# A causal and sink-window attention feeding a two-matmul FFN: one explicit list of pieces in place of generated interleaving

## The chip, the cores and the metric

The kernel runs on one core of one Trainium2 chip. The metric is device microseconds of one execution, as the median of several. Before the change it is 242.58 us (three runs, 242.34 to 242.89). The profile that is read below is one execution with a span of 241.1 us from the first to the last instruction.

Names used throughout: TensorE (PE) multiplies matrices, VectorE (DVE) and ScalarE (ACT) work on tiles and read the matmul results out of PSUM, GpSimd (POOL) works on tiles in SBUF and starts some transfers, SyncE (SP) starts most transfers. Each engine takes its instructions in the order in which the program lists them for it.

## The reference

Four batches, eight heads, 768 tokens, head size 64. Heads 0, 2 and 6 are "retrieval" heads with full causal attention. The others are "streaming" heads: a token sees the first four tokens and the last 64. The attention output of all heads is then put through an FFN of width 512, 2048, 512 with a PReLU between.

```python
scores = scale * np.matmul(q, k.transpose(0, 1, 3, 2))
rel = pos[:, None] - pos[None, :]
causal = rel >= 0
stream_keep = causal & (is_sink | (rel < window))       # n_sink = 4, window = 64
mask = np.where(is_retrieval, causal, stream_keep)      # per head
a = softmax(np.where(mask, scores, -1e9))
x = np.matmul(a, v)        # transposed and reshaped to (3072, 512)
h = x @ w_in               # (3072, 2048)
g = np.maximum(h, 0.0) + alpha * np.minimum(h, 0.0)
out = g @ w_out            # (3072, 512), float32
```

Inputs are float32; the kernel casts to bfloat16 and accumulates in float32.

## The kernel before

Heads are handled in 16 pairs n: four pairs per batch, in the order (0, 1), (2, 3), (6, 7), (4, 5). For the first eight pairs q and k are transposed on TensorE; for the others a transfer transposes them. The FFN takes tokens in eight groups t, of 512 and 256 tokens alternately, two per batch.

The pieces, cut to what matters:

```python
# PSUM: 8 banks of 128 x 512 float32, by fixed roles
BANK = {"sc0": 0, "sc1": 1, "mm2": 2, "m2": 3, "mm0": 4, "mm1": 5, "m0": 6, "m1": 7}

def Tq(n):      # transpose q of both heads (6 matmuls), then copy to qT
    tr = T_bank(natq.pop(n), ...)
    nc.scalar.copy(qT[n % NK][:, 0:S]..., in_order(tr[:, 0:S], T))          # L301

def Tk(n):      # transpose k of both heads (6 matmuls), then copy to kT, head by head
    ...         # copies: L314 (retrieval heads), L320 to L322 (streaming heads)

def S_retr(n, hh, m):                    # scores of a retrieval head, piece m
    ... nc.tensor.matmul(sc..., kt..., qt..., stop=not masked)              # L362
        if masked:   # n < 4: add -30000 where not causal, by a matmul
            nc.tensor.matmul(sc..., ident, nmr..., start=False, stop=True)  # L365
    nc.scalar.activation(e..., sc..., AF.Exp, scale=scale)                  # L370
    ... nc.vector.tensor_tensor(ej, ej, mask, op=ALU.mult)   # n >= 4       # L375

def S_stream(n, hh, m):                  # scores of a streaming head
    on_pe = n < 3 or n == 3 and hh == 1
    ... nc.tensor.matmul(sc..., kt..., qt..., start=True, stop=not on_pe)   # L393
        if on_pe:
            nc.tensor.matmul(sc..., ident, nms..., start=False, stop=True)  # L396
    nc.scalar.activation(slots, sc..., AF.Exp, scale=scale)                 # L400
    if not on_pe:
        nc.vector.tensor_tensor(slots, slots, factor, op=ALU.mult)          # L404
# n >= 8 has a streaming form of its own: L412, L415, L419, L420, L422

def AV(n, hh):                           # attention times values, then normalise
    ... nc.tensor.matmul(pav[:, i, :], e..., vv...)          # 27 or 13     # L467
    nc.vector.reciprocal(rcp, pav[:, :, D:D + 1])                           # L472
    nc.vector.tensor_tensor(xn[n]..., pav..., rcp..., op=ALU.mult)          # L473

def X(n):                                # transpose the output: TensorE or a transfer
    ... nc.tensor.transpose(tr..., nat[:, i, :], ident)      # 7            # L486
    nc.vector.tensor_copy(xT[:, n % 4, o:o + S], tr[:, 0:S])                # L487

def P1(t, f, cs=range(4), where=""):     # first FFN matmul: 4 or 8 matmuls per piece
    ... nc.tensor.matmul(psg..., w_in_b..., xT[:, c, o:o + w])   # c: pair  # L516
    nc.scalar.activation(neg, psg, AF.Relu, scale=-1.0)                     # L523
    nc.vector.scalar_tensor_tensor(g_buf..., neg..., oma..., psg...)        # L526

def P2(t, s, quarter, where=""):         # second FFN matmul: 4 matmuls per quarter
    ... nc.tensor.matmul(bank(po[t, s]), g_buf..., w_out_b[:, f, :])        # L536
    if quarter == 3:
        nc.scalar.copy(ot, bank(po.pop((t, s))))                            # L541
        (nc.gpsimd if t < 6 else nc.sync).dma_start(out[r:r + 128, :], ot)
```

Each piece issues its matmuls and what ScalarE and VectorE do with them in one go, so the order of pieces is the order of all engines. The order comes from loops. Batch 0 (n < 4) is written out, with 36 warming matmuls ahead of it:

```python
whole_q(0); whole_k(0)
for i in range(36):
    nc.tensor.matmul(warm[:, 0:128], ident, ident, start=True, stop=True)
Tq(0); Tk(0)
...
for n in range(4):      # scores of pair n, with AV and X of pair n - 1 and Tq, Tk of n + 1 between
    ...
AV(3, 1)
LEAD = 4
for f in range(2):
    P1(0, f, range(3), where="lead")     # over the pairs 0 to 2, before X(3)
X(3)
for f in range(2, LEAD):
    P1(0, f, range(3), where="lead")
nc.vector.tensor_scalar(mr, nmr, 0.0, None, op0=ALU.is_equal)               # L663
...                                      # the rest of P1(0, ...)
```

From pair 4 on, `seg_pieces(n)` gives the attention pieces of a pair, and FFN pieces of earlier tokens are laid between them by a budget, evenly from one batch's end to the next. Loads of pair n + 4 follow in a pair's loop, on SyncE; the weights are loaded by GpSimd in eight transfers after the casts of batch 0.

Of the kernel before, what the change touches and what calls it, by code (L numbers as in the profile page):

```python
# [8 lines left out]
AF = mybir.ActivationFunctionType  # L9
ALU = mybir.AluOpType  # L10
DT = mybir.dt


@with_exitstack
def kernel(
# [60 lines left out]
    BANK = {"sc0": 0, "sc1": 1, "mm2": 2, "m2": 3, "mm0": 4, "mm1": 5, "m0": 6, "m1": 7}  # L76

    def bank(tag):
        return P[:, BANK[tag], :]

    def bank_bf(tag):
        return P[:, BANK[tag], :].bitcast(bf16)

# [80 lines left out]
    def load(n):  # L164
        load_q(n)
        load_k(n)
        load_v(n)

    natq, natk = {}, {}
# [7 lines left out]


    def whole_q(n):
        nat = natq[n] = NAT0[0][n] if n < 4 else NATQ[n % 2]  # L180
        copy = nc.gpsimd.tensor_copy if 0 < n < 6 else nc.scalar.copy if 0 < n < CROSS else nc.vector.tensor_copy
        flat = qf[n % NF].rearrange("p a b d -> p (a b d)")[:, 0:12 * D]
        copy(nat.rearrange("p i (h d) -> p h i d", h=2), flat.rearrange("p (h i d) -> p h i d", h=2, d=D))
        if n >= CROSS:
            nc.sync.dma_start(qT[n % NK][:, 0:S].rearrange("p (i r) -> p i r", r=128),
                              nat.rearrange("p i c -> p (i c)"), transpose=True)

    def whole_k(n):
        if n < CROSS:
            natk[n] = NAT0[1][n] if n < 4 else NATK1[n % 2]  # L190
            for hh, h in enumerate(heads(n)):
                copy = nc.gpsimd.tensor_copy if 0 < n < 6 else nc.scalar.copy if n == hh == 0 else nc.vector.tensor_copy

                T = row_tokens(n, h)
                flat = kf[n % NF].rearrange("p a b d -> p (a b d)")[:, 6 * D * hh:6 * D * (hh + 1)]
                copy(natk[n][:, :, D * hh:D * (hh + 1)].rearrange("p (t i) d -> p t i d", t=T),
                     flat.rearrange("p (i t d) -> p t i d", t=T, d=D))
            return
        flat = NATK[n % 2]
        rows = flat.rearrange("p (h x) -> p h x", h=2)[:, :, 0:896].rearrange("p h (t c) -> p h t c", c=128)  # L200
        nc.vector.tensor_copy(rows[:, :, :, 0:D], kf[n % NF].rearrange("p t h d -> p h t d"))
        sinks(n, rows)
        for hh, h in enumerate(heads(n)):
            nt = 6 if RETR[h] else 7
            nc.sync.dma_start(kTs[n % NK][hh][:, 0:128 * nt].rearrange("p (i r) -> p i r", r=128),
                              flat[:, 896 * hh:896 * hh + 128 * nt], transpose=True)

    def whole_v(n):
        vv = vb[n % NV]
        (nc.gpsimd if n < 6 else nc.vector).tensor_copy(vv[:, :, :, 0:D], vf[n % NF])  # L210
        sinks(n, vv.rearrange("p t h c -> p h t c"))

    for i in range(NF):
        nc.vector.memset(vf[i][:, 6, :, :], 0.0)
    load_q(0)
    load_k(0)
    alpha_r = wpool.tile([16, 128], fp32, name="alpha_r")
    nc.scalar.dma_start(alpha_r, moe_alpha.rearrange("(a p) -> a p", p=128))
    for n in range(1, 4):
        load_q(n)  # L220
        load_k(n)
        load_v(n - 1)
    load_v(3)

    zero = const.tile([128, 1], bf16, name="zero")
    nc.vector.memset(zero, 0.0)
    one = const.tile([128, 1], bf16, name="one")
    nc.vector.memset(one, 1.0)
    ident = const.tile([128, 128], bf16, name="ident")
    make_identity(nc, ident)  # L230
    ident_f = const.tile([16, 16], fp32, name="ident_f")
    mr = const.tile([128, 5, 144], bf16, name="mr")
    mr_near = const.tile([128, 6, 208], bf16, name="mr_near")

    ms_near = const.tile([128, 3, 176], bf16, name="ms_near")
    ms = const.tile([128, 2, 192], bf16, name="ms")
    ms5 = const.tile([128, 2, 192], bf16, name="ms5")
    nmr = const.tile([128, 5, 144], bf16, name="nmr")
    nms = const.tile([128, 192], bf16, name="nms")
    nms6 = const.tile([128, 44], bf16, name="nms6")  # L240
    OUT = -30000.0


    nc.gpsimd.affine_select(nms, zero.to_broadcast([128, 192]), pattern=[[-1, 192]], base=63,
                            channel_multiplier=1, compare_op=ALU.is_ge, fill=OUT)
    nc.gpsimd.memset(nms[0:NSINK, 0:128], 0.0)
    nc.gpsimd.affine_select(nms, nms, pattern=[[1, 192]], base=0,
                            channel_multiplier=-1, compare_op=ALU.is_ge, fill=OUT)

    nc.gpsimd.tensor_copy(nms6, nms[:, 0:44])  # L250
    nc.gpsimd.memset(nms6[0:NSINK, 0:NSINK], OUT)

    nc.gpsimd.affine_select(nmr, zero.unsqueeze(1).to_broadcast([128, 5, 144]), pattern=[[-4, 5], [1, 144]], base=0,
                            channel_multiplier=-1, compare_op=ALU.is_ge, fill=OUT)

    nc.scalar.copy(kT_all[:, 2].rearrange("p h c -> p (h c)"), zero.to_broadcast([128, 2 * 7 * 128]))
    nc.vector.memset(kT_all[:, 0].bitcast(fp32), 0.0)
    nc.vector.memset(qT_all[:, :, S:S + 32].bitcast(fp32), 0.0)
    nc.gpsimd.memset(kT_all[:, 3].bitcast(fp32), 0.0)
    nc.vector.memset(kT_all[:, 1].bitcast(fp32), 0.0)  # L260
    nc.vector.memset(vb_all[:, :, :, :, D:D + 1], 1.0)
    ONES = 1.001937866210937
    nc.vector.memset(eR_all[:, :, FAR.RTOT:E_R].bitcast(fp32), ONES)
    eSv = eS_all[:, :, 0:6 * SLOT].rearrange("p n (s c) -> p n s c", c=SLOT)
    for i in range(NS):
        nc.vector.memset(eSv[:, i, :, 192:SLOT].bitcast(fp32), 0.0)
    nc.vector.memset(eS_all[:, :, 5 * SLOT + 192:6 * SLOT + 128].bitcast(fp32), ONES)
    nc.vector.tensor_copy(ident_f, ident[0:16, 0:16])

    w_in_b = wpool.tile([128, 4, d_ff], bf16, name="w_in_b")  # L270
    w_out_b = wpool.tile([128, 16, d_model], bf16, name="w_out_b")
    oma = wpool.tile([128, 16], fp32, name="oma")

    def load_w_in(lo, hi):
        nc.gpsimd.dma_start(w_in_b[:, :, lo:hi], moe_w_in[:, lo:hi].rearrange("(a p) f -> p a f", p=128))

    def load_w_out(n):
        nc.gpsimd.dma_start(w_out_b[:, 4 * n:4 * n + 4, :],
                            moe_w_out[512 * n:512 * (n + 1), :].rearrange("(a p) f -> p a f", p=128))


    n_misc = [0]

    def misc_tag():
        n_misc[0] += 1
        return f"m{n_misc[0] % 2}"

    def T_bank(nat, tag):
        tr = bank_bf(tag)
        for i in range(6):  # L290
            nc.tensor.transpose(tr[:, 128 * i:128 * (i + 1)], nat[:, i, :], ident)  # L291
        return tr
# [5 lines left out]
    def Tq(n):  # L298
        tr = T_bank(natq.pop(n), "mm0" if n < 4 else misc_tag())
        T = row_tokens(n)  # L300
        nc.scalar.copy(qT[n % NK][:, 0:S].rearrange("d (p t) -> d p t", t=T), in_order(tr[:, 0:S], T))  # L301

    def Tk(n):
        tr = T_bank(natk.pop(n), "mm1" if n < 4 else misc_tag())
        for hh, h in enumerate(heads(n)):
            T = row_tokens(n, h)
            rows = slice(64 * hh, 64 * hh + 64)
            kt = kTs[n % NK][hh][rows, :]
            src = in_order(tr[rows, 0:S], T)
            copy = nc.scalar.copy if n >= 4 and hh == 0 else nc.vector.tensor_copy  # L310
            if RETR[h]:
                cuts = [0, -(-256 // T), S // T] if n == 0 else [0, S // T]
                for lo, hi in zip(cuts, cuts[1:]):
                    copy(kt[:, 0:S].rearrange("d (p t) -> d p t", t=T)[:, lo:hi, :], src[:, lo:hi, :])  # L314
                continue
            slots = kt.rearrange("d (j m t) -> d j m t", j=7, t=T)
            a, first, z, last = NSINK // T, NSINK // T, 748 // T, 128 // T
            if n >= LAY:
                first, z, last = 0, 672 // T, 116 // T
            copy(slots[:, 0:6, a:last, :], src[:, first:z, :].rearrange("d (j m) t -> d j m t", j=6))  # L320
            nc.vector.tensor_copy(slots[:, 6, a:a + S // T - z, :], src[:, z:S // T, :])
            nc.vector.tensor_copy(slots[:, :, 0:a, :], src[:, 0:a, :].unsqueeze(1).to_broadcast([64, 7, a, T]))  # L322

    ebuf = {}
    n_e = [0, 0]

    def take_e(n, hh):
# [441 lines left out]
```

The softmax here doesn't subtract the row's maximum and nothing guards it: scores larger than these inputs give would overflow.

## Time and profile before

| what | value |
|---|---|
| time, median of 3 | 242.58 us (242.34 to 242.89) |
| span in the profile | 241.1 us, TensorE clock 1.000 |
| first transpose of real data | 5.69 us |
| last matmul ends | 237.80 us |
| costliest line of VectorE: L526 (PReLU) | 74.6 us busy, 128 pieces |
| costliest line of ScalarE: L523 (its ReLU) | 57.3 us busy, 96 pieces |
| costliest lines of TensorE: L516, L536 (FFN) | 95.4 and 92.0 us busy |
| moved by transfers | 36.25 MB, 90,513 packets |

How to read the views: a line of the groups gives the source line, engine, operation, the tiles with their shapes, a count, then the busy time, the mean length of one in ns, and the idle time of the engine just before it. The windows give every engine's busy time in a stretch of time. The waits give for which engine and line one engine stood idle. The chain of work that ended last goes backwards from the last instruction, at each step to what released it. Matmuls are pipelined: the mean length of one (379 ns for 512 columns) is more than the distance from its start to the next one's start.

### The profile page before, as it was taken

Reading aid. Unit: us, or ns where it says so; the run is one execution under the profiler, and the core shown is the slowest. Engines: PE = TensorE matmul, PEld = TensorE weight load, DVE = VectorE, ACT = ScalarE, POOL = GpSimd, SP = SyncE. Lnnn points to the kernel's source line nnn. Section 1 sums busy time; section 2 is a strip of 40 time slices with the busy share of each in tenths; the row PEclk is TensorE's granted clock in tenths of the full one; section 3 lists DMA queues with packets and bytes.
Section 4 is the critical chain, followed back from the end, with each engine's and each line's share of the span. In section 5 each row is a group of like instructions: output and inputs, shape, how many; then the busy total and the mean of one; then the engine's idle time right before and its main releaser. Section 6 shows DMA issues by size and latency. Waiting matters only on the chain.

```text
span 241.1 us, 5264 instructions
## 1 busy us (share of the span) xinstructions
PE 229.2 (95%) x2017; PEld 144.1 (60%) x2017; DVE 165.5 (69%) x405; ACT 144.1 (60%) x265; POOL 43.7 (18%) x90
## 2 busy tenths in 40 slices
PE   7799799989987999999999999999999999999994
PEld 6688545566756655455666655556666544465553
DVE  7688889768788867989577858884665465633410
ACT  5788358957855756776655557866564254523220
POOL 5668950641110100000000000000000000000000
PEclk9999999999999999999999999999999999999999
DMA  6999999999999999999999991603131101011112
GB/s 212 292 251 169 232 202 201 244 251 254 251 224 162 196 244 211 217 162 245 164 238 168 219 169 59 126 3 77 46 78 44 46 0 45 0 59 74 44 44 90
DMA packets 90513, 36.25 MB, mean 150 GB/s; under 512 B 77672, under 2 KB 88696, under 8 KB 90488
## 3 DMA queue, kind: packets, MB, share of 16 engines
q1 hardware_dynamic: 84504, 26.66, 56.9%
q0 software_dynamic: 5664, 8.91, 16.6%
q10 hardware_dynamic: 320, 0.34, 0.6%
q8 instruction: 16, 0.26, 0.5%
q14 instruction: 9, 0.07, 0.1%
HBM read 27.55 MB, written 6.29 MB: 140 GB/s over the span
## 4 chain that ended last, share of the span: by engine, by line
PE 84%; DVE 7%; ACT 6%; issue 1%; ACTq 0%; DVEq 0%
PE P L516 34%; PE P L536 31%; PE P L467 6%; PE P L362 5%; ACT eR L370 2%; PE P L412 2%; PE P L291 2%; ACT eS L400 2%; PE P L553 1%; DVE xn L473 1%; PE P L486 1%; DVE eS L404 1%; DVE g L526 1%; PE P L393 1%; ACT neg L523 1%
## 5 line engine op out<-in xcount | busy, mean ns | idle before, releaser
L526 DVE SCALAR_TENSOR_TENSOR g<-neg,oma,P 128x512 bf16<-128x512 f32 (+1 forms) x128 | 74.6, 610 | 43.2 <-ACT neg L523 41.6
L516 PE MATMUL P<-xT,w_in_b 128*128 128x512 bf16 (+1 forms) x512 | 95.4, 326 | 0.0
L536 PE MATMUL P<-w_out_b,g 128*128 128x512 bf16 x368 | 92.0, 379 | 0.0
L523 ACT ACTIVATE neg<-P 128x512 f32<-128x512 f32 x96 | 57.3, 598 | 51.5 <-PE P L516 46.9
L516 PEld LDWEIGHTS <-w_in_b 128*128 128x128 bf16 x512 | 48.0, 98 | 29.3 <-issue 0.5
L536 PEld LDWEIGHTS <-g 128*128 128x128 bf16 x368 | 33.9, 98 | 30.1
L370 ACT ACTIVATE eR<-P 128x488 bf16<-128x488 f32 (+4 forms) x63 | 38.4, 620 | 13.9 <-PE P L362 11.8
L544 POOL DMA_DIRECT2D out_dram<-ot x18 | 9.8, 544 | 134.0 <-ACT ot L541 134.0
L362 PE MATMUL P<-qT,kT 128*128 128x488 bf16 (+17 forms) x132 | 24.7, 273 | 1.5 <-ACT eS L400 0.6
L473 DVE TENSOR_TENSOR xn<-P,rcp 128x448 bf16<-128x448 f32 x32 | 20.0, 624 | 1.1
L541 ACT COPY ot<-P 128x512 f32<-128x512 f32 x23 | 13.5, 587 | 9.0 <-PE P L536 8.6
L362 PEld LDWEIGHTS <-kT 128*128 128x128 bf16 x132 | 11.5, 98 | 10.0 <-issue 0.8
L415 ACT ACTIVATE eS<-P 128x352 bf16<-128x352 f32 x30 | 13.9, 462 | 5.7 <-PE P L412 5.7
L400 ACT ACTIVATE eS<-P 128x384 bf16<-128x384 f32 (+1 forms) x25 | 13.2, 558 | 4.6 <-PE P L393 4.0
L467 PE MATMUL P<-vb,eS 128*128 128x65 bf16 x260 | 11.7, 193 | 2.5 <-DVE eS L404 1.3
L467 PEld LDWEIGHTS <-eS 128*128 128x128 bf16 x260 | 10.5, 97 | 5.3 <-DVE eS L404 1.5
L467 PEld LDWEIGHTS <-eR 128*128 128x128 bf16 x324 | 11.4, 97 | 2.5 <-DVE eR L375 0.9
L467 PE MATMUL P<-vb,eR 128*128 128x65 bf16 x324 | 12.1, 192 | 0.8 <-DVE eR L375 0.8
L375 DVE TENSOR_TENSOR eR<-eR,mr_near 128x128 bf16<-128x128 bf16 (+5 forms) x36 | 8.2, 240 | 6.7 <-ACT eR L370 6.7
L420 DVE TENSOR_TENSOR eS<-eS,ms_near 128x352 bf16<-128x352 bf16 x30 | 10.1, 338 | 3.8 <-ACT eS L415 3.6
L393 PE MATMUL P<-qT,kT 128*128 128x192 bf16 (+2 forms) x70 | 10.0, 234 | 0.8 <-ACT eR L370 0.6
L412 PEld LDWEIGHTS <-kT 128*128 128x128 bf16 x70 | 6.6, 98 | 6.4
(97 smaller groups left out, 187.3 us busy)
## 6 DMA issues: line engine op xcount, KB each, us to landing
qf<-in_q_dram SPq DMA_DIRECT2D x16, 384.0 KB
out_dram<-ot POOLq DMA_DIRECT2D x18, 256.0 KB, 3.1
vf<-in_v_dram SPq DMA_DIRECT2D x22, 192.0 KB
kf<-in_k_dram SPq DMA_DIRECT2D x21, 192.0 KB
w_in_b<-in_moe_w_in_dram POOLq DMA_DIRECT2D x4, 512.0 KB, 8.3
w_out_b<-in_moe_w_out_dram POOLq DMA_DIRECT2D x4, 512.0 KB, 19.9
kf<-in_k_dram SPq DMA_DIRECT2D x9, 196.0 KB
vf<-in_v_dram SPq DMA_DIRECT2D x9, 196.0 KB
```

The lines of the kernel that those rows point to most:

```text
L362: nc.tensor.matmul(sc[:, x, a - lo:z - lo], kt[:, 128 * j:128 * (j + 1)], qt[:, c:c + z - a], start=True, stop=not masked)
L370: nc.scalar.activation(e[:, lo:hi].rearrange("p (x c) -> p x c", x=len(parts)), sc[:, 0:len(parts), 0:(hi - lo) // len(parts)], AF.Exp, sc ...
L393: nc.tensor.matmul(sc[:, x, o:o + w], kt[:, 128 * j:128 * (j + 1)], qt[:, 124 * j:124 * j + w], start=True, stop=not on_pe)
L400: nc.scalar.activation(slots, sc[:, 0:len(thirds), 0:384].rearrange("p x (s c) -> p x s c", c=192), AF.Exp, scale=scale)
L415: nc.scalar.activation(slots, sc[:, 0:352].rearrange("p (s c) -> p s c", c=176), AF.Exp, scale=scale)
L467: nc.tensor.matmul(pav[:, i, :], e[:, o:o + 128], vv[:, j, hh, 0:D + 1], start=(m == 0), stop=(m == len(terms) - 1))
L473: nc.vector.tensor_tensor(xn[n][:, :, 64 * hh:64 * hh + 64], pav[:, :, 0:D], rcp.to_broadcast([128, NT, D]), op=ALU.mult)
L516: nc.tensor.matmul(psg[:, w * i:w * (i + 1)], w_in_b[:, a, 128 * fb:128 * (fb + 1)], xT[:, c, o:o + w], start=(c == 0), stop=(c == 3))
L523: nc.scalar.activation(neg, psg, AF.Relu, scale=-1.0)
L526: nc.vector.scalar_tensor_tensor(g_buf[t % 2][:, fb, 0:w], neg[:, c], oma[:, fb:fb + 1], psg[:, c], op0=ALU.mult, op1=ALU.add)
L536: nc.tensor.matmul(bank(po[t, s]), g_buf[t % 2][:, f, 128 * s:128 * (s + 1)], w_out_b[:, f, :], start=(f == 0), stop=(f == 15))
L541: nc.scalar.copy(ot, bank(po.pop((t, s))))
```

## The change

The pieces are split so that what TensorE does (capital letters in the list) and what ScalarE or VectorE does with the result (small letters) are separate items. All items, 1,063 of them, are called in the order of one list, which is written out. The order on each engine thus no longer follows from the order on another. PSUM banks are taken from a pool, by which was free longest, instead of by fixed roles.

Along with this:

- All masks of batch 0 are added on TensorE, also that of pair 3's first head.
- The first pair is loaded (q), cast, transposed and copied head by head.
- 26 warming matmuls instead of 36.
- The first six pieces of the first FFN matmul go in three parts: pairs 0 and 1, pair 2, pair 3.
- The mask factors mr (for L375) are built at the start rather than after batch 0.
- Loads, casts and mask building stand in the list too, so weights and pairs are loaded in another order.

The purpose is to keep TensorE busy where it waited for the other engines.

The core of the diff; the list is cut to its beginning and two later stretches:

```diff
+ORDER = """
+id zero kz3 qz0 nmr Lq0.0 sz2 Lk0 Ck0.1 warm kz0 ro Lq1 kz2 kz1 Lq0.1 Cq0.0 Tq0.0 Ck0.0 vo Cq1 gate mr Lk1 vz0 Cq0.1
+Lq2 vz1 La sz1 idf Tk0.0 tq0.0 tk0.0 Ck1.0 Tk0.1 S0.0.2 S0.0.0 Lv0 Tq0.1 s0.0.2 Lk2 Ck1.1 qz S0.0.1 tk0.1 Tk1 tq0.1
 ...
+S2.0.2 s2.1.1 Lk4 X1 tk3.0 wi1 x1 s2.0.2 S2.1.0 s2.1.0 A2.0 S3.0.1 nz1 Lq4 tk3.1 A2.1 Cv3 S3.0.0 wi2 Ck4.0 s3.0.1
+s3.0.0 a2.0 a2.1 P0.3.0 Lk5 S3.1.0 S3.1.1 X2 wi3 P0.2.0 Cq4 s3.1.1 one A3.0 x2 P0.1.0 s3.1.0 A3.1 P0.1.1 kfz2 P0.0.0
+P0.0.1 P0.3.1 Lv4 a3.0 P0.5.0 Ck4.1 a3.1 X3 ms P0.4.0 P0.2.1 P0.5.1 x3 P0.0.2 P0.4.1 p0.0 g0.0 P0.5.2 P0.3.2 nr p0.5
 ...
+g4.2 g4.11 p4.12 S14.0.4 a12.1 Lk15 m13.0.1 s14.0.4 O3.1.0 S14.1.1 Dq15 m13.0.0 P5.2 S14.0.0 P4.14 g4.12 m14.1.0 A13.0
 ...
+""".split()
 ...
-    BANK = {"sc0": 0, "sc1": 1, "mm2": 2, "m2": 3, "mm0": 4, "mm1": 5, "m0": 6, "m1": 7}
+    def take(*choices):
+        got = min((c for c in choices if all(age[b] >= 0 for b in c)), key=lambda c: max(age[b] for b in c))
+        for b in got:
+            age[b] = -1
+        return got
 ...
+    MISC = [(6,), (7,)]
+    SC = [(0,), (1,)]
+    SC2 = [(0, 1), (2, 3)]
+    FF = [(2,), (3,), (4,), (5,)]
+    LEAD = [(4,), (5,), (3,), (2,), (0,), (1,)]
+    TAIL = [(b,) for b in (2, 3, 4, 5, 0, 1, 6, 7)]
 ...
-        on_pe = n < 3 or n == 3 and hh == 1
 ...
+                nc.tensor.matmul(sc[:, x, o:o + w], kt[:, 128 * j:128 * (j + 1)],
+                                 qt[:, 124 * j:124 * j + w], start=True, stop=n >= 4)
+                if n < 4:
+                    nc.tensor.matmul(sc[:, x, o:o + w], ident, (nms6 if j == 6 else nms)[:, 0:w],
+                                     start=False, stop=True)
 ...
-        for i in range(36):
+        for i in range(26):
 ...
+    for i in range(2):
+        item(f"Lq0.{i}", nc.sync.dma_start, part_of(qf[0], i), dram(q, i * S * D, [[6 * D, 128], [1, 6 * D]]))
+        item(f"Cq0.{i}", cast_q0, i)
+        item(f"Tq0.{i}", lambda i=i: to_array(("q0", i), natq[0], MISC, i == 0))
+        item(f"tq0.{i}", put_q, ("q0", i), 0, slice(D * i, D * i + D), "AV"[i])
+        item(f"Tk0.{i}", lambda i=i: to_array(("k0", i), natk[0], [(4,), (5,)], i == 0))
+        item(f"tk0.{i}", put_k, ("k0", i), 0, i)
 ...
+            if t == 0 and f < 6:
+                for part, cs in enumerate((range(0, 2), range(2, 3), range(3, 4))):
+                    item(f"P0.{f}.{part}", P1, 0, f, cs, LEAD)
 ...
+    for name in ORDER:
+        I[name]()
```

The items: L loads, C casts, T and t transposes and their copies, S, s and m scores, exponentials and masks, A and a attention times values and its normalisation, X and x the transposes of the output, P, p and g the first FFN matmul, its ReLU and its PReLU, O and o the second FFN matmul and its copy out, wi and wo the weights. S4.1.2 is pair 4, second head, third piece; P0.3.1 is token group 0, piece 3, second part.

## The prediction

> **What bounds the kernel now.** I read the page first: busy shares, then the forty slices.
>
> ```profile
> PE 229.2 (95%) x2017; PEld 144.1 (60%) x2017; DVE 165.5 (69%) x405; ACT 144.1 (60%) x265; POOL 43.7 (18%) x90
> PE   7799799989987999999999999999999999999994
> ```
>
> A slice is 6.03 us. TensorE (PE) is full from the fourteenth slice on and has holes before. The busy share hides most of a hole, because a matmul's modelled end lies about 0.17 us after the next could have started. So I looked at start-to-start times instead, in the chain of work that ended last (start, length, what):
>
> ```profile
> 13.06 0.81 PE P L467 x27
> 80.61 0.87 PE P L516 x8
> 82.04 0.86 PE P L536 x4
> ```
>
> That is 30 ns for 65 columns, 109 ns for 256 and 216 ns for 512: columns divided by 2.4 GHz plus about 2.4 ns[...].
>
> This gives an account of the span. Summed over the groups by shape, the 2017 matmuls have 521,056 columns: 217.1 us, and 2017 x 2.4 ns adds 4.8. I count 222.4, because those under 65 columns don't fall below some 28 ns. The 36 warming matmuls (4,608 columns, 2.0 us) lie ahead of the first transpose, at 5.69 us. So 220.4 us of needed work stands between 5.69 and the last matmul's end at 237.80, which is 232.1 us. **TensorE idles 11.7 us in between**; another 3.3 us at the end are the last copy and store.
>
> Where? The same stages in the windows (length; busy and count by engine; clock; DMA share; GB/s):
>
> ```profile
> 5.60:30.60 25.00, 21.45 (x340) 18.33 (x341) 19.35 (x49) 16.80 (x23) 19.58 (x35) 1.00 1.13 237
> 30.60:42.00 11.40, 11.40 (x65) 5.47 (x63) 10.88 (x15) 8.14 (x14) 3.00 (x9) 1.00 1.22 199
> 42.00:78.00 36.00, 32.50 (x350) 22.30 (x349) 28.98 (x82) 25.80 (x50) 8.92 (x18) 1.00 1.14 231
> 78.00:187.00 109.00, 109.00 (x943) 66.19 (x942) 81.08 (x210) 70.04 (x142) 7.02 (x13) 1.00 0.79 148
> ```
>
> Start-to-start excess over 0.1 us adds up to about 5.3 us in the first stage (attention of batch 0), nothing in the second (first matmul of the FFN), about 4.9 in the third (batch 1), and one 0.14 us hole afterwards; the rest is the small per-matmul excess. The waits of TensorE, for 0 to 30 us and 42 to 78 us, name the causes (waited for: total, times, longest):
>
> ```profile
> PE P L467 <- DVE xn L473: 1.2, 2, 1.0
> PE P L393 <- ACT eR L370: 0.6, 1, 0.6
> PE P L362 <- DVE kT L314: 0.5, 1, 0.5
> ...
> PE P L467 <- DVE eS L404: 1.3, 2, 0.8
> PE P L486 <- DVE xn L473: 0.9, 1, 0.9
> PE P L467 <- DVE eR L375: 0.8, 1, 0.8
> ```
>
> These are queues on VectorE (DVE) and ScalarE (ACT) that stand in program order, not an engine at its limit: in 42 to 78 us DVE is 80% busy. The largest is around the only mask of batch 0 that VectorE still multiplies:
>
> ```profile
> 24.46 1.61 DVE L404 TENSOR_TENSOR eS<-eS,ms 128x768 bf16<-128x768 bf16 x1 [0.47 <-ACT eS L400]
> 26.00 0.19 DVE L472 RECIPROCAL rcp<-P 128x7 f32<-128x7 f32 x1
> 26.22 0.62 DVE L473 TENSOR_TENSOR xn<-P,rcp 128x448 bf16<-128x448 f32 x1
> ```
>
> The outputs of pair 2 have to queue behind 1.61 us of masking for pair 3; TensorE has a hole of 1.16 us before 26.91, then 0.61 and 0.37.
>
> **What the Trainium skill says.** "TensorE: Matmul & The Clock Gate", section "Back-to-back issue gap", gives N/2.4 + 2.5 ns for a warm array; the trace agrees (216 ns at 512). The same page, section "Architectural detail: the array is 16× 32×32, not 1× 128×128", has ScalarE and VectorE as strict first-in first-out; the lines just shown fit. "SBUF — State Buffer", section "SBUF: two separate sides", says VectorE and GpSimd exclude each other on a shared port pair. The 768-wide mask at 1.61 us, against 0.366 us for a 384-wide one, ran while GpSimd issued weight transfers (24.35 to 27.3 us), which agrees in direction. "Trace analysis", section "Identifying the Most-Contended Engine", says matmul busy time misleads: here 95% with 11.7 us idle.
>
> **The change, part by part.**
>
> *Work.* The mask of pair 3's first head goes to TensorE: 7 matmuls, 1,152 columns. The first pair is transposed head by head: 12 more transposes, 1,536 columns. Ten warming matmuls go: 1,280 columns, in time that is idle anyway. Needed work rises by 2,688 columns, 1.12 us, and 19 x 2.4 ns: **plus 1.2 us**, to 221.6. VectorE loses 1.61 and 0.36 us of masking, and gains one 64-partition copy of 768 columns (0.94 us by the L314 row).
>
> *Start.* The first q transfer is halved and its cast covers half the columns, so the first transpose may come around 5.3 us instead of 5.69: minus 0.4. But building all of mr (1.96 us at 31.46) now precedes the first kT copy on VectorE, so part of this may be lost.
>
> *Batch 0.* Scores, exponentials, outputs and copies get separate places in the list, so engines no longer share one order of pieces. Into the holes go FFN parts of the first token tile over two pairs, then one, then one: some 2.8 us of matmuls stand ahead of X(3), against 1.3 before. But VectorE has about 20 us between its first kT copy and the last output of pair 3: five stream-head kT copies at 1.28, three others at 0.94 to 1.09, one qT copy at 0.94, eight outputs at 0.82, three xT copies at 0.55, small fills. From 6 us that ends at 26 without any wait, or 28 at 90%. TensorE's own list puts X(3) 21.3 us after the first transpose, at 26.6. So 1.5 to 2.5 us of idle stay here of 5.3: **minus 3.3**.
>
> *Batch 1.* The first scores are moved between the pieces of the first matmul, and masks and PReLU pieces are placed apart from the scores that feed them. In TensorE's new list 3 us or more of its own work stand between a pair's last scores and the value matmuls that use them (3.1 for S4.1.2 to A4.1, 5.0 for S7.1.2 to A7.1), against a chain of 0.56 (exponential) + 0.24 to 0.37 (mask). I leave 2 us of 4.9: **minus 2.9**.
>
> *Later.* Attention of batches 2 and 3 comes earlier: in TensorE's list X(15) stands 164 us after the first transpose, at about 174 us, against 187.9. VectorE's 164.4 us then fall more thickly: some 143 before that point, 84% on average (77% before), over 90% in stretches. I add **plus 1.0** for holes that the kernel before doesn't have.
>
> Sum: 242.58 + 1.2 - 0.4 - 3.3 - 2.9 + 1.0 = 237.2. I go a little below, to **236.4 us**, because the list looks placed to fill even the small holes. The floor with no hole: 5.3 + 221.6 + 3.3 = 230.2 of span, and 1.5 more as in the measured time (242.58 against a span of 241.1): 231.7.
>
> **Rivals.** (1) *VectorE becomes the bound.* If its queue, at over 90% in stretches, runs late, banks and masks come late and holes reappear between 80 and 165 us. For it: the second stage already has VectorE at 10.88 of 11.40 us. Against: over whole stages it has room. With 4 us lost so: 240. (2) *Transfers become the bound.* SyncE issues without pause from 54 to 142 us, and the DMA engines are full in the same slices; the list now needs the scores of pairs 8 to 15 some 10 to 20 us earlier. w_out is issued behind a cast that waits for pair 5's keys. For it: 12.4 MB had moved by 54 us, and the new list needs a similar amount by then. Against: it defers values and brings keys and queries forward. If it holds: 241 to 244. (3) *Nearly all holes vanish:* 233 to 234, if the list was fitted to durations like these and the chip keeps to them. (4) *Only the mask and the start matter* and new holes replace the old: 240 to 241.
>
> **Range and chances.** My sum leaves about 5 us of idle. A factor of two in it, and one moderate transfer or VectorE wait, gives 233.0 to 240.8. Faster by over 2% means below 237.7, so at most 6 us of idle: 0.60. Within 2%: 0.37. Slower: 0.03, which would need transfers to hold up TensorE by over 12 us more than now.
>
> **What would show it.** Right: no wait on L404 masks before 30 us, X(3) starting by 28 us, start-to-start excess in 42 to 78 us at half or less, the last scores by 165 us, VectorE's busy sum at 164 to 165, TensorE's count 9 higher. Wrong: waits of transposed keys or of w_out on transfers (rival 2), repeated waits for g or eS after 80 us (rival 1), or holes in batch 0 still summing to 5 us, which would mean that ScalarE's and VectorE's sums, not their order, set that stage.

## The result, and the profile after

The changed kernel takes 239.64 us in the median (four runs, 238.58 to 240.62), against 242.59: a ratio of 0.988 (0.985 to 0.991). It is faster by 2.95 us, where 6.2 were forecast. The profiled execution took 240.62 us, with a span of 238.9 us. Its trace lacks the records of 29 of the 2026 matmuls (x1997 in the first line below), each of which looks like a hole of 0.22 us; counts of weight loads (PEld) are complete, and such holes are left out of the sums here.

The page, busy shares and the rows of TensorE and its clock in forty slices (5.97 us each):

```profile
PE 227.6 (95%) x1997; PEld 143.7 (60%) x2026; DVE 161.0 (67%) x404; ACT 138.9 (58%) x265; POOL 44.8 (19%) x92
...
PE   7799879999999999999999999999999999999994
...
PEclk9999979999999999999999999999999999999999
```

In the kernel before TensorE had holes up to the thirteenth slice. Now they are gone from the seventh slice on, but the sixth, around 30 to 36 us, is new, and there alone the row of TensorE's clock is below full.

The windows of the changed kernel, cut at the new hole (length; busy and count by engine; clock; DMA share; GB/s):

```profile
4.30:24.00 19.70, 17.79 (x299) 15.24 (x299) 16.15 (x45) 15.36 (x21) 13.70 (x27) 1.00 1.07 251
24.00:37.00 13.00, 10.57 (x95) 6.55 (x96) 9.74 (x18) 3.97 (x8) 11.14 (x26) 0.87 1.19 255
37.00:78.00 41.00, 40.62 (x384) 27.03 (x388) 34.55 (x95) 33.34 (x66) 6.89 (x12) 1.00 0.88 176
```

From 37 us on TensorE is full, with GpSimd (fifth pair of numbers) busy for only 6.89 of 41 us. From 24 to 37 us GpSimd is busy for 11.14 of 13 us, ScalarE for only 3.97, and TensorE is idle for 2.4 us and loses, at a mean clock of 0.87, another 13.00 x 0.13 = 1.7 us.

What TensorE waited for longest over the whole span (total, times, longest):

```profile
PE P L543 <- DMA w_in_b<-in_moe_w_in_dram: 2.3, 1, 2.3
```

It is one wait of the first FFN matmul for the second quarter of w_in; no other after the first transpose is above 0.7 us. The timeline of TensorE around it (start, length, what, in brackets the idle time before and its releaser):

```profile
31.51 0.61 PE L543 MATMUL P<-xT,w_in_b 128*128 128x512 bf16 x2 [2.33 <-DMA w_in_b<-in_moe_w_in_dram]
31.95 0.84 PE L523 MATMUL P<-ident,xn 128*128 128x128 bf16 x7
```

and its weight loads, one of which stands ahead of each matmul:

```profile
33.02 0.15 PEld L543 LDWEIGHTS <-w_in_b 128*128 128x128 bf16 x1 [0.28 <-issue]
33.45 0.15 PEld L543 LDWEIGHTS <-w_in_b 128*128 128x128 bf16 x1 [0.28 <-issue]
```

X(3), the seven transposes (L523), begins at 31.95 us. After the wait the 512-column matmuls follow each other at 0.43 us instead of 0.216, until about 35.5 us. That is half clock, and it takes away the prediction's 216 ns for 512 columns while it lasts. It is not in every execution: the four had mean clocks of 0.993, 1.000, 0.991 and 1.000 with 240.62, 238.58, 239.84 and 239.44 us.

VectorE and GpSimd in the same time:

```profile
28.93 4.00 DVE L603 TENSOR_SCALAR ms<-nms 128x192 bf16<-128x192 bf16 x2
...
33.58 0.55 DVE L528 COPY xT<-P 128x768 bf16<-128x768 bf16 x1
```

```profile
29.66 0.22 POOL L278 MEMSET kf<- 128x128 f32 x1
29.81 0.51 POOL L318 CAST natm<-kf 128x384 bf16<-128x384 f32 x1
30.27 1.26 POOL L614 TENSOR_SCALAR_AFFINE_SELECT mr_near<-one 128x1248 bf16<-128x1248 bf16 x1
31.48 0.90 POOL L278 MEMSET natk<- 128x960 f32 x1
```

Two instructions of 192 columns (item `ms` of the list, factors that are first used in batch 1) take 4.00 us on VectorE, while GpSimd goes from one instruction to the next without a pause. Behind them stands the last copy of batch 0's outputs (L528, item `x3`), which ends at 34.13 us. So two things come late at once: the weights, at 31.47 us, and that copy. The wait table names only the one that TensorE met first.

### The profile page after: what moved, and what is told of

Same layout as the page of the kernel before. It is cut to its first block, busy times and chain, and to the rows that moved or that the text cites. A ratio compares the mean times of both kernels' runs of the same rounds, so it can differ in the third digit from the quotient of the medians.

```text
span 238.9 us, 5226 instructions
## 1 busy us (share of the span) xinstructions
PE 227.6 (95%) x1997; PEld 143.7 (60%) x2026; DVE 161.0 (67%) x404; ACT 138.9 (58%) x265; POOL 44.8 (19%) x92
## 4 chain that ended last, share of the span: by engine, by line
PE 78%; DMA 9%; SPq 5%; POOL 3%; issue 2%; DVE 1%; ACT 0%; POOLq 0%
PE P L543 33%; PE P L563 29%; PE P L501 5%; DMA w_in_b<-in_moe_w_in_dram 4%; PE P L405 4%; DMA vf<-in_v_dram 3%; PE P L438 2%; PE P L579 1%; DMA kf<-in_k_dram 1%; PE P L348 1%; PE P L523 1%; SPq L517 1%; PE P L444 1%; POOL vb L333 1%; SPq L232 1%
## 5 line engine op out<-in xcount | busy, mean ns | idle before, releaser
L543 PE MATMUL P<-xT,w_in_b 128*128 128x256 bf16 (+1 forms) x501 | 94.2, 328 | 3.5 <-DMA w_in_b<-in_moe_w_in_dram 2.3
L555 DVE SCALAR_TENSOR_TENSOR g<-neg,oma,P 128x256 bf16<-128x256 f32 (+1 forms) x128 | 72.6, 610 | 35.5 <-ACT neg L548 34.9
L563 PE MATMUL P<-w_out_b,g 128*128 128x512 bf16 x350 | 85.9, 379 | 1.0
L548 ACT ACTIVATE neg<-P 128x512 f32<-128x512 f32 x96 | 55.1, 604 | 42.9 <-PE P L543 40.5
L543 PEld LDWEIGHTS <-w_in_b 128*128 128x128 bf16 x512 | 48.8, 98 | 32.8 <-issue 2.9
L563 PEld LDWEIGHTS <-g 128*128 128x128 bf16 x368 | 34.6, 98 | 33.5 <-DVE g L555 0.2
L405 PE MATMUL P<-qT,kT 128*128 128x280 bf16 (+16 forms) x132 | 23.6, 272 | 0.8 <-DVE kT L368 0.7
L511 DVE TENSOR_TENSOR xn<-P,rcp 128x448 bf16<-128x448 f32 x32 | 20.0, 625 | 1.1
L405 PEld LDWEIGHTS <-kT 128*128 128x128 bf16 x132 | 10.9, 97 | 7.9 <-DVE kT L368 0.8
L510 DVE RECIPROCAL rcp<-P 128x7 f32<-128x7 f32 x32 | 6.4, 201 | 5.2 <-PE P L501 5.0
L438 PE MATMUL P<-qT,kT 128*128 128x176 bf16 (+1 forms) x70 | 9.4, 234 | 0.0
```

The costliest lines, as they stand in the source:

```text
L405: nc.tensor.matmul(sc[:, x, a - lo:z - lo], kt[:, 128 * j:128 * (j + 1)], qt[:, c:c + z - a], start=True, stop=not masked)
L438: nc.tensor.matmul(sc[:, 0, 176 * x:176 * x + w], kt[:, 128 * j:128 * (j + 1)], qt[:, 112 * j:112 * j + w], start=True, stop=True)
L511: nc.vector.tensor_tensor(xn[n][:, :, 64 * hh:64 * hh + 64], pav[:, :, 0:D], rcp.to_broadcast([128, NT, D]), op=ALU.mult)
L543: nc.tensor.matmul(psg[:, w * i:w * (i + 1)], w_in_b[:, a, 128 * fb:128 * (fb + 1)], xT[:, c, o:o + w], start=(c == 0), stop=(c == 3))
L548: nc.scalar.activation(neg[t, f], bank(held["P", t, f][0]), AF.Relu, scale=-1.0)
L555: nc.vector.scalar_tensor_tensor(g_buf[t % 2][:, fb, 0:w], neg[t, f][:, c], oma[:, fb:fb + 1], bank(got[0])[:, c], op0=ALU.mult, op1=ALU.add)
```

## The experiments

My theory: the gain is missing between 28 and 36 us, where the list put a transfer and five small VectorE instructions too close ahead of the matmuls that need them. Rival: what the separate sequences of the engines bring is small in itself, and the gain comes from the mask and the start. Every kernel was timed beside the kernel before on the same chip; the ratio is to that. The ratio leaves out executions over 1.5% above the fastest of their kernel (ten of 20 of the one with the matmuls moved, at most one of any other), the medians and ranges leave out none. Edits are of the list of the changed kernel, unless said otherwise.

### Weights earlier

```diff
- ... so Cv1 wi0 tk1.1 ... X1 tk3.0 wi1 x1 ...
+ ... so wi0 Cv1 wi1 tk1.1 ... X1 tk3.0 x1 ...
```

> The changed kernel with the first two w_in slices moved one place forward on GpSimd (the first before the cast of pair 1's values, the second where the first was); no other engine's list changes. Theory (the wait for the second slice, 2.5 us, and the half clock that follows it, some 1.7 us, ate the gain): TensorE no longer waits for w_in before 32 us, the clock stays 1.00, the time falls from 239.6 to 236 to 237. Rival (transfers are a bound; the wait only moves): a wait of about the same size appears for another transfer and the time stays above 239. Second rival (ScalarE and VectorE set the end of batch 0 anyway): the wait goes, but X(3) starts no earlier than now minus 1 us, and the time falls by 1 us at most.

Measured: 241.06 us (239.69 to 243.02), ratio 0.995 (0.992 to 0.997): slower than the changed kernel. Its waits of TensorE:

```profile
PE P L543 <- DVE xT L528: 2.8, 1, 2.8
PE P L501 <- POOL vb L333: 1.6, 1, 1.6
```

The wait for w_in is gone, and in its place the first matmuls over pair 3 wait 2.8 us for the copy behind `ms`. The earlier weights were also not free: GpSimd's cast of pair 2's values starts at 22.50 us after a wait of 3.90 us, where it started at 19.55 us without one, and TensorE waits 1.6 us for it. In this stage the DMA engines have no room left (DMA share 1.07 to 1.19 in the windows of the changed kernel).

### The matmuls that need the second quarter, later

```diff
- ... P0.5.0 Ck4.1 a3.1 X3 ms P0.4.0 P0.2.1 P0.5.1 x3 P0.0.2 P0.4.1 p0.0 g0.0 P0.5.2 P0.3.2 nr p0.5 P0.4.2 ...
+ ... Ck4.1 a3.1 X3 ms P0.2.1 x3 P0.0.2 p0.0 g0.0 P0.3.2 P0.5.0 P0.5.1 P0.4.0 P0.4.1 P0.5.2 P0.4.2 nr p0.5 ...
```

> The changed kernel with the six parts of the first FFN matmul that need the second w_in slice moved behind X(3) and the last parts of the pieces 0 and 3; transfers as they are. Theory of the wait: 1.4 us of other work comes into the hole, so the wait shrinks to about 1 us, the clock may stay high, and the time falls to 237 to 238. Rival (transfers set the end of the stage): the same time as the changed kernel, within 0.5 us, as the slice lands no earlier. Second rival (X(3) must wait for VectorE in any case): X(3) starts at 29 us or later and 0.5 us is gained.

Measured: 240.62 us (236.85 to 243.22), ratio 0.986 (0.983 to 0.989), not told apart from the changed kernel. The wide range goes with the clock: six of the 20 executions had a mean clock of 0.997 or more and took 236.85 to 239.86 us, the other 14 had 0.985 to 0.993 and took 239.94 to 243.22. TensorE in the profiled one (0.990):

```profile
32.34 3.91 PE L543 MATMUL P<-xT,w_in_b 128*128 128x512 bf16 x10 [3.13 <-DVE xT L528]
```

VectorE:

```profile
28.29 2.63 DVE L603 TENSOR_SCALAR ms<-nms 128x192 bf16<-128x192 bf16 x2
```

X(3) came 3.5 us earlier, at 28.43, but the copy of its result still stood behind `ms` and started at 31.74 us. In the profiled executions of these two edits each cause alone keeps the hole, and half clock follows (10 matmuls in 3.91 us).

### The wait filled with work that nobody needs

```diff
- ... Lv4 a3.0 P0.5.0 Ck4.1 ...
+ ... Lv4 a3.0 fill P0.5.0 Ck4.1 ...   # 40 matmuls of 128 columns
```

> The changed kernel with 40 matmuls of 128 columns that compute nothing needed (some 2.2 us) just before the first matmul that waits for the second w_in slice. Theory that half of the loss is the clock: the wait for the transfer is replaced by this filler, the clock stays 1.00 in every run, and the time is 238 to 238.8, near the lowest runs of the changed kernel (238.58) and without its spread. Rival (the clock has no part, the lower record is chance): the time is the same as now, 239.6, or up to 0.3 us longer.

Measured: 238.86 us (238.17 to 240.62), ratio 0.987 (0.982 to 0.992). TensorE:

```profile
29.32 2.40 PE L648 MATMUL P<-ident 128*128 128x128 bf16 x40
...
32.59 1.89 PE L543 MATMUL P<-xT,w_in_b 128*128 128x512 bf16 x8
```

Real work resumes at the same moment, 31.55 us, and then at full clock (8 matmuls in 1.89 us). All four executions had a mean clock of 1.000, against two of four of the changed kernel, and against seven and six of 20 at 0.997 or more with the two edits above. So the half clock comes from the idle time. In the medians the filler can't be told from the changed kernel, which goes to half clock only in some executions.

VectorE and GpSimd in the same execution:

```profile
29.22 0.59 DVE L603 TENSOR_SCALAR ms<-nms 128x192 bf16<-128x192 bf16 x2
...
30.15 1.29 DVE L606 COPY ms<-ms 128x148 bf16<-128x148 bf16 x1
```

```profile
30.13 1.25 POOL L614 TENSOR_SCALAR_AFFINE_SELECT mr_near<-one 128x1248 bf16<-128x1248 bf16 x1
```

The two factors took only 0.59 us here: they ran beside casts and a short memset and ended before GpSimd's affine select began. The copy behind them met it and lasted as long as it did. So which instruction of `ms` is stretched, and by how much, depends on what GpSimd runs just then; in all, to the end of the last copy, `ms` takes 3.1 us here and 4.6 us in the changed kernel.

### Mask factors later, alone and with each of the two other edits

```diff
- ... a3.1 X3 ms P0.4.0 ... s4.1.2 Ck6.0 m4.1.0 ...
+ ... a3.1 X3 P0.4.0 ... s4.1.2 Ck6.0 ms m4.1.0 ...
```

> The changed kernel with the five VectorE instructions that build the mask factors ms and ms5 moved from before the last xT copy of batch 0 (where GpSimd works without pause; they took 4.7 us there) to just before the first mask that reads them, at about 50 us, where GpSimd is idle. Theory A (the shared port locks VectorE out, so xT comes 4 us late): the five take under 1.2 us, the last xT copy ends by 30 us instead of 34.1. The second w_in slice is still waited for until 31.5, so alone it gives 0.5 to 1.5 us: 238 to 239. Theory B (only the w_in slice counts): no change in time, 239.6, as now.

Measured: 237.73 us (237.00 to 238.16), ratio 0.979 (0.974 to 0.984). The two instructions of `ms`, by shape, in this kernel (minimum, median, maximum ns; first and last start):

```profile
L603 DVE TENSOR_SCALAR ms<-nms x2: 203/204/204, 48.6 to 48.8; 128x192 bf16<-128x192 bf16 x2
```

They now take 0.41 us together instead of 4.00. What is left of the wait is the weights: TensorE waits 1.35 us for them before 31.14 us, and the matmuls after it run at full clock (9 in 2.11 us; all four executions had 1.000).

With the second edit added, nothing should be left:

> Both: the mask factors late, and the six parts that need the second w_in slice behind X(3) and the last parts. Theory A with the slice as second cause: the hole at 29 to 32.5 us shrinks to 1.5 us or less, the clock stays at 1.00, and the time is 235 to 236.5, the sum that the prediction made. Theory B: 237.5 to 238.5, as with the other order alone. Transfers as a bound: another wait for a transfer takes over and the time stays above 238.5.

Measured: 236.80 us (236.33 to 237.07), ratio 0.976 (0.972 to 0.980), the fastest kernel of this study. TensorE, VectorE and the windows:

```profile
29.75 2.32 PE L543 MATMUL P<-xT,w_in_b 128*128 128x512 bf16 x10 [0.43 <-DVE xT L528]
```

```profile
29.14 0.56 DVE L528 COPY xT<-P 128x768 bf16<-128x768 bf16 x1 [0.66 <-PE P L523]
```

```profile
24.00:37.00 13.00, 12.41 (x111) 7.61 (x113) 8.49 (x16) 7.55 (x14) 12.08 (x27) 1.00 1.19 250
```

X(3) starts at 28.54 us, its copy at 29.14, and the clock stays full. TensorE is busy for 12.41 of the 13 us, against 10.57.

The last variant keeps the mask factors late and brings the weights earlier instead:

> Both: the mask factors late, and the first two w_in slices one place earlier. If the values' transfer competes with the weights (the earlier slices alone cost 1.6 us of waiting for pair 2's values, cast 3 us later): 237.5 to 239, about 2 us better than the earlier slices alone (241.06) and no better than the mask factors alone. If only the mask factors hid the gain of the earlier slices: 235.5 to 236.5.

Measured: 237.81 us (237.46 to 239.79), ratio 0.982 (0.977 to 0.988). The hole is gone here as well, but TensorE waits 1.0 us for values, as with the earlier weights alone. GpSimd's cast of pair 2's values starts at 22.38 us here and at 22.50 with the earlier weights alone, but between 18.95 and 20.05 us in the profiled executions of the changed kernel and of the other edits of its list (the two that tie the engines together aside). Of the two ways to let the weights come in time, the one that leaves the transfers alone is no worse, and by the medians better.

### GpSimd's masks moved instead of VectorE's

```diff
- ... P0.5.2 P0.3.2 nr p0.5 ... P0.6 g0.3 ns P0.1.2 ... m5.1.2 wo3 S5.1.0 ...
+ ... P0.5.2 P0.3.2 p0.5 ... P0.6 g0.3 P0.1.2 ... m5.1.2 wo3 nr ns S5.1.0 ...
```

> The changed kernel with the mask factors where it has them, but GpSimd's building of the near masks (14 instructions, 5 us, in 30 to 36 us) moved behind its last weight transfer, where it idles. If GpSimd's port use is what stretches the mask factors on VectorE from 0.2 to 2 us each: the five take less than 2.5 us instead of 4.7, the last xT copy ends 2 us earlier, 238 to 239. If something else stretches them (an engine that they wait for): 4 us and more as now, 239.6.

Measured: 238.26 us (237.03 to 239.66), ratio 0.983 (0.979 to 0.988). VectorE:

```profile
28.75 0.87 DVE L603 TENSOR_SCALAR ms<-nms 128x192 bf16<-128x192 bf16 x2
...
29.96 0.97 DVE L606 COPY ms<-ms 128x148 bf16<-128x148 bf16 x1
```

`ms` stands at its old place, and only GpSimd's work beside it changed. GpSimd:

```profile
29.92 0.95 POOL L278 MEMSET natk<- 128x960 f32 x1
```

The two factors fall from 4.00 to 0.87 us. What is left of GpSimd's work still stretches them and the copies: the 148-column copy runs from 29.96 to 30.93 us, beside GpSimd's memset from 29.92 to 30.87; it takes 0.19 us at 49 us in the kernel with `ms` late, where GpSimd is idle. To the end of the last copy `ms` takes 2.2 us, where it took 4.6. So the length of these instructions is GpSimd's doing. The time itself isn't told apart from the changed kernel's. "SBUF — State Buffer", section "SBUF: two separate sides", has the port pair that the two share as an exclusive lock, and the traces agree in kind; the section gives no size for what happens beside an unbroken row of GpSimd instructions, which here is up to a factor of ten.

Both edits together, on top of the fastest kernel:

> The best kernel so far (mask factors late, parts that need the second w_in slice behind X(3): 236.8) with GpSimd's near masks late as well. If GpSimd's queue holds up the casts and the w_out transfers behind it: up to 0.5 us faster, 236.3. Otherwise the same, 236.8.

Measured: 237.40 us (236.85 to 240.44), ratio 0.979 (0.976 to 0.982). With `ms` out of the way, moving GpSimd's masks brings nothing more.

### Each engine's work tied back to TensorE's

The order of TensorE, transfers and casts is kept. Each item of ScalarE or VectorE (`s`, `m`, `a`, `x`, `p`, `g`, `o`) stands directly behind the matmuls that feed it, or behind the last reader of the buffer that it writes. A stretch of the list (of the second version below):

```diff
- P0.11 S4.0.1 g0.10 p0.11 S4.0.0 g0.6 Lk6 P0.9 P0.12 g1.0 s4.0.1 g0.11 s4.0.0
+ P0.11 p0.11 g0.11 S4.0.1 s4.0.1 S4.0.0 s4.0.0 m4.0.0 m4.0.1 Lk6 P0.9 p0.9 g0.9 P0.12 p0.12 g0.12
```

In the first version some masks of retrieval heads stood ahead of one of the two exponentials that they cover, so a part of the masking is left out.

> The changed kernel with TensorE's list, transfers and casts as they are, but each exponential, mask, normalisation, ReLU, PReLU and copy put directly behind the matmuls that feed it (or behind the last reader of the buffer that it writes), as in the kernel before. It takes away the separate sequence of each engine and keeps the order on TensorE. Theory (separate sequences took away the holes of batch 1): start-to-start excess in 42 to 78 us comes back, 3 to 5 us, and the time is 243 to 245. Rival (the order on TensorE alone did it, by laying 3 us and more between a score and its use): the time stays within 1 us of 239.6.

Measured: 257.22 us (254.78 to 259.16), ratio 1.058 (1.051 to 1.065). In the second version each such mask stands behind both exponentials, and nothing is left out:

> As the glued kernel before, with each mask of a retrieval head put behind both exponentials that feed it. The mend changes the place of a few masks on VectorE only, so the time should be that of the first glued kernel, 255 to 259. Theory (separate sequences hold this order up): far above the kernel before. Rival (the misplaced masks caused the loss): 240 to 245.

Measured: 257.00 us (255.92 to 257.68), ratio 1.059 (1.054 to 1.065). Its waits of TensorE:

```profile
PE P L501 <- DVE vb L333: 6.0, 5, 2.3
PE P L438 <- DMA kT<-natk: 3.8, 3, 2.0
```

The order of TensorE alone is not worth keeping: without the separate orders of the other engines it costs 17 us, far more than the 3 to 5 us expected. The holes of batch 1 are back: from 42 to 78 us TensorE is busy for 31.77 us at a mean clock of 0.91, against 35.68 at 1.00 in the changed kernel and 32.50 at 1.00 in the kernel before. Casts of values and the transfers of keys behind casts come late, presumably because one engine's queue now holds work that waits for TensorE ahead of work that TensorE will wait for; that was not tested by itself. This speaks against the first half of the rival theory, but doesn't settle it: the run doesn't say what separate sequences would bring to the order of the kernel before. Nor was it tested what the pool of PSUM banks contributes; all kernels with the list have it.

### The mask alone, in the kernel before

```diff
-        on_pe = n < 3 or n == 3 and hh == 1
+        on_pe = n < 4
```

> The kernel before with one part of the change: the mask of pair 3's first head on TensorE (7 matmuls more, 0.5 us), the two VectorE multiplications (1.61 and 0.36 us) away. Theory of the prediction (the outputs of pair 2 queue behind them, holes of 1.16, 0.61 and 0.37 us): 1.0 to 1.6 us faster, 241 to 241.6. Rival (VectorE's sum sets the end of batch 0, or the transfers do, so that a wait of another kind follows): within 0.4 us of 242.6.

Measured: 242.02 us (241.21 to 243.71), ratio 1.000 (0.998 to 1.001). The windows are cut as in the prediction; the third stage:

```profile
42.00:78.00 36.00, 32.74 (x347) 21.98 (x346) 28.82 (x83) 24.34 (x48) 8.92 (x18) 1.00 1.11 235
```

In the first stage TensorE does more (22.55 us busy against 21.45), but batch 1 keeps its holes, with 32.74 of 36 us busy against 32.50. In this profiled execution X(3) starts at 28.87 us instead of 30.39 and the span is 240.0 us instead of 241.1, as the theory has it; over 20 executions the mean gain is under 0.5 us. Why the mean shows nothing of it stays open. The wait for the mask was the largest hole in sight, and removing it by itself made no measurable difference. Of the rival's second half, the mask falls with this; the start is left.

### The first q in one piece

The fastest kernel, but q of the first pair is loaded, cast, transposed and copied whole, as in the kernel before:

```diff
- ... Lq0.0 ... Lq0.1 Cq0.0 Tq0.0 ... Cq0.1 ... tq0.0 ... Tq0.1 ... tq0.1 ...
+ ... Lq0.0 ... Cq0.0 Tq0.0 ... tq0.0 ...          # each for both heads
```

> The best kernel so far with the first pair's q loaded, cast, transposed and copied in one, as in the kernel before (k stays head by head). If the halved transfer brought the earlier start (first transpose at 4.36 us instead of 5.69): the first transpose comes at 5 us or later and the time is 0.5 to 1 us longer, 237.3 to 237.8. If the fills, now behind the first casts on VectorE, brought it: the first transpose stays before 4.8 us, and the time is 236 to 236.8, since six transposes, one copy of 0.94 us and a 0.8 us hole go as well.

Measured: 237.57 us (236.34 to 238.24), ratio 0.980 (0.976 to 0.984), 0.8 us above the fastest in the medians, with overlapping intervals. TensorE at the start:

```profile
5.49 0.82 PE L348 MATMUL P<-ident,g 128*128 128x128 bf16 x6 [1.11 <-DVE g L305]
...
8.19 0.56 PE L405 MATMUL P<-qT,kT 128*128 128x106 bf16 x2 [0.35 <-DVE kT L368]
```

TensorE in the fastest kernel:

```profile
4.31 1.49 PE L346 MATMUL P<-ident,g 128*64 128x128 bf16 x12
...
6.90 0.37 PE L405 MATMUL P<-qT,kT 128*128 128x106 bf16 x2 [0.45 <-DVE kT L368]
```

The halved transfer is there before the warming matmuls end, so the first transpose starts 1.18 us earlier in the fastest kernel (4.31 against 5.49 us), and its first scores 1.29 us earlier (6.90 against 8.19 us). In the profile that is nearly the whole of the change's gain at the start (1.33 us); the medians give 0.8 us of it.

The two executions differ in something else, too: when TensorE comes to full clock. Six transposes of 128 columns, first in the kernel with q in one piece, then in the fastest:

```profile
7.02 0.82 PE L348 MATMUL P<-ident,g 128*128 128x128 bf16 x6
```

```profile
7.99 0.50 PE L348 MATMUL P<-ident,g 128*128 128x128 bf16 x6
```

They follow each other at 107 ns (half clock) against 56. In the profile with q in one piece this lasts until 12.0 us, in that of the fastest kernel until about 6.2, in that of the changed kernel until 4.8 (the page's clock row doesn't show it). So a part of the 0.8 us can be the clock's and not the transfer's.

## Why the prediction was wrong

The time lies inside the range, at 239.64 of 233.0 to 240.8, but 6.2 us of gain were forecast and 2.95 came. A part of that is arithmetic: the terms of the prediction add up to -4.4, so to 238.2 us and not to 237.2 (the +1.0 for later holes isn't in its sum), and from there to 236.4 there is no term, only the remark that the list looks placed to fill even the small holes. The terms, as measured in the profiled execution:

| term | predicted, us | measured, us | how |
|---|---|---|---|
| TensorE's needed work | +1.2 | +1.2 | 2026 weight loads, 9 more, as counted |
| start | -0.4 | -1.3 | first transpose at 4.36, not 5.69 |
| batch 0 | -3.3 | +2.0 | 3.1 (4.4 to 24 us) + 2.5 + 1.7 (24 to 37 us) = 7.3, against 5.3 |
| batch 1 | -2.9 | -4.9 | no start-to-start excess left between 37 and 78 us |
| later | +1.0 | +0.7 | one wait at 145.4 us |
| end | 0 | +0.3 | last copy and store 3.55, not 3.29 |

Measured, this adds up to -2.0; the span fell from 241.1 to 238.9, by 2.2. The median fell by a little more than the profiled execution, which was the longest of the four.

**The step that failed is the term for batch 0**, -3.3 predicted and +2.0 measured: "VectorE has about 20 us between its first kT copy and the last output of pair 3 ... From 6 us that ends at 26 without any wait, or 28 at 90%", and from it 1.5 to 2.5 us of idle. The sum was nearly right for what it held: the last output of pair 3 (L511) runs from 28.38 to 29.00 us. But two items were not in it. `ms` stands in the list between `X3` and `x3`, and I took it for one of the "small fills"; in the kernel before the two factors took 0.4 us at 12.7 us, but here they met GpSimd's busiest stretch and took 4.00. And `wi1` starts the second quarter of w_in at 20.84 us, while P0.5.0, which reads it, stands ahead of X(3). The transfer took 10.63 us. I looked at when engines get to their work, and not at when the weights get to it. With both put right, X(3) starts at 28.54 us and the time is 236.80: 2.8 of the 3.2 us that were missing.

That this comes so close to 236.4 is in part luck. The term was too hopeful before the two items, too: from 4.4 to 24 us there are already 3.1 us of idle, more than the prediction left for the whole stage. The longest waits there, 0.7 us for VectorE's copy of the first keys (L368) and 0.6 us for GpSimd's cast of the second half of the first q (L309), have nothing to do with the two items. The fastest kernel's profile keeps 2.2 us there and 0.6 from 24 to 37 us, so its batch 0 gains 2.5 us and not 3.3. It is batch 1, the start and the missing holes later on, all better than predicted, that make up for it. The prediction also gave a sign of being wrong, holes in batch 0 still summing to 5 us, and it came (3.1 + 2.5); but what it was to mean, that the sums of ScalarE and VectorE set the stage and not their order, is refuted by the fastest kernel, where order alone halves them.

**Start**: the direction was right, the size was not. The 1.96 us for mr, which I feared, became 0.50 us at 4.30 us, where GpSimd was idle. It looks like the same effect as with `ms`, this time in the kernel's favour.

**Batch 1**: right in mechanism, and the size was too careful. The list left no hole where I kept 2 us.

**Later**: VectorE is not a bound. Its busy time is 161.0 us, not 164 to 165, and after 78 us the trace shows one wait of TensorE for it, 0.56 us for g. The last scores, though, come at about 168 us, not by 165, with the whole shifted by the hole. Rival 1 didn't happen.

**Rivals**: rival 2 was right that a transfer takes the place of a wait, but named w_out and the later keys, and those came in time. The one that was late was w_in. Rival 4, new holes for old, came nearest in its number. Rival 3, nearly no holes, holds from 37 us on. With the two items moved, about 5.2 us of idle are left: 226.8 us from the first transpose at 4.31 us to the last matmul's end at about 231.1, less 221.6.

**The mask**: the prediction called it the largest hole, which it was. That its removal alone brought nothing measurable in the mean shows that the size of a hole isn't what its removal brings. The prediction saw in the 1.61 us of this mask the lock between VectorE and GpSimd, since GpSimd was issuing weight transfers. The trace doesn't bear that out: the 384-wide mask at 26.77 us, beside the same issues (24.35 to 27.30 us), took 0.35 us, as such masks do elsewhere (median 0.351). What stretched the wide one stays open.

**TensorE's work**: right. The prediction's columns divided by 2.4 GHz plus 2.4 ns holds again (216 ns at 512 columns, with a weight load ahead of each), but only at full clock: in the hole it was 0.43 us.

## What to carry to other kernels

When a list gives every engine its own order, check each item for two times: when its engine gets to it, and when the last transfer that it needs has landed; an FFN piece pulled forward into a hole pulls its weights forward too. Work of VectorE that is needed only later should not stand ahead of a copy that TensorE waits for, above all not beside an unbroken row of GpSimd instructions. Where two causes come late together, the wait table names only the first, and removing one may show nothing (the weights here) or a part of the gain (`ms`): test them together as well.

## What the runs showed of the hardware that was not expected

- Small VectorE instructions can be stretched tenfold by GpSimd: two of 192 columns took 0.41 us with GpSimd idle, 0.59 and 0.87 us beside casts and a short memset, and 2.63, 3.36 and 4.00 us beside casts, memsets and an affine select in a row. A copy of 148 columns took 0.19 us with GpSimd idle and 1.29 us beside an affine select of 1.25 us.
- Half clock came after a shorter idle time than expected. "TensorE: Matmul & The Clock Gate", section "What's actually happening", gives an idle window of about 3.4 us; here idle times of 2.3, 2.8 and 3.1 us were followed by half clock in the profiled executions, 3.4 us of it in the changed kernel (a mean clock of 0.66 from 31 to 36 us), and idle times of 1.35 and 1.09 us were not. The measurement decides, and it varied between executions of the same kernel.
- A quarter of w_in took 10.63 us from issue to landing while other transfers were under way, and issuing it 4.9 us earlier (with the first quarter 2.9 us earlier) put off the cast of pair 2's values by 3 us (22.50 against 19.55 us).
